# A long convolution beside a gated MLP, backward pass: halo rows moved by DMA, and one slab load placed later

## The chip, the cores and the metric

The kernel runs on one core of a Trainium2 chip. The metric is the device time of one execution in microseconds (us); lower is better. The engines are TensorE (PE in the profile, PEld for its weight loads), VectorE (DVE), ScalarE (ACT), GpSimd (POOL) and SyncE (SP), which here issues most of the DMAs ("SPq" rows are such issues).

## What is computed

The reference is the forward pass and the gradients of a block with two branches on one layer-normed input, S = 2048 positions, D = 1024 channels, F = 3584 hidden columns, all bf16.

```python
def _A_ref(q, k, v, shift_k, ssm_k, ssm_D):
    k_pad = jnp.pad(k, ((0, 0), (ks - 1, 0), (0, 0)))          # ks = 4 taps
    for t in range(ks):
        k_shift = k_shift + k_pad[:, t:t + S, :] * shift_k[:, ks - 1 - t][None, None, :]
    kv = k_shift * v
    y = ...                        # causal convolution of kv with ssm_k along S, by FFT
    y = y + kv * ssm_D[None, None, :]
    return q * y
def _B_ref(x, W_gate, W_up, W_down):
    gate = x @ W_gate;  gate = gate * (gate > 0);  h = gate * (x @ W_up)
    return h @ W_down

x = A_q
xn = _layernorm(x, axis=-1)
out = x + _A_ref(xn, A_k, A_v, ...) + _B_ref(xn, W_gate, W_up, W_down)
# returned: out, and by jax.vjp the gradients of A_q, A_k, A_v, shift_k, ssm_k, ssm_D and the three weights
```

What matters here is the gradient through the four-tap shift. With gks the gradient of k_shift, the gradient of k at position s is the sum over i of gks[s + i] * shift_k[i], i = 0 to 3. It needs the next three positions; behind the last position they are zero.

## The kernel before, in words

**The MLP branch** (class LnMlp) has four phases of large matmuls. `hidden` makes gate, up and the hidden gradients, 14 blocks of 512 columns (two halves of the rows, seven column blocks each), with weight tiles wg, wu and wdT refilled from HBM ahead of the next block (`load_gate`, `load_up`, `load_down`). The results h and the two gradients ug are stored to the HBM scratch tensors h_d and ug_d. `grad_down` makes the gradient of W_down from slabs of h (tile hs) and the output gradient (g_nat), and `grad_in` makes those of W_gate and W_up from slabs of ug (tile ugs) and the normed input (xn_nat). A slab is 2048 rows by 512 columns, 2 MB, loaded by eight DMAs of 256 KB into one of two sets of buffers (`slab`, `slab_part`, L1216 to L1230). `grad_in` runs 14 turns of 128 matmuls. At the start of turn k it asks for the slab of turn k + 1. Behind them come `out_phase` and `grad_x`, the forward output and the gradient of the input.

At the change from grad_down to grad_in the last columns of the one and the first of the other are computed by `four` (L1244): four PSUM banks are accumulated together, first over the rows 0 to 7 (blocks of 128) and then over 8 to 15. In grad_down's last `four` each g_nat block that has been read for the last time gives its buffer to an xn_nat block (`load_xn`, L1289), so the last eight xn_nat loads can be issued only when grad_down's last matmuls have run. Stores of finished tiles (wo of grad_down, wi of grad_in) are deferred by two steps (`defer`, `tick`).

**The convolution branch** (class ABranch) handles the channels in eight groups of 128. Per group it does forward and inverse transforms by matmuls, with elementwise products on VectorE. A group in time layout is a tile of 128 partitions by 19 rows by 128 channels. Partition 64u + q holds the 16 consecutive positions from 32q + 16u on in its rows 0 to 15; so the position behind the last one of a partition is row 0 of another partition: partition 64 + q for q in the first half, and q + 1 of the first half for 64 + q. Rows 16 to 18 of the tile gks are the halo: a copy of rows 0 to 2 of that next partition. `halo` (L493) fills them, and `taps` reads rows i to i + 15 for tap i. `tap_sums`, the sums for the gradient of shift_k, reads rows 0 to 15 only.

**Order.** Once the convolution branch has started (`pri.strict`), every instruction of an engine is kept in the order in which the program emits it, DMA issues on SP too. The MLP phases are generators that yield after every 8 matmuls or so with an estimated time. The convolution branch is a list of slots (`slots`, L627), each with a PE part and a VectorE part. The main loop gives it slots until their estimated times have used up what the MLP phase has yielded. In `hidden` a slot counts 1900 ns; in the dense phases (grad_down, grad_in) it counts 1900 ns with a PE part and 1250 ns without:

```python
    SLOT, DENSE = 1900, (1900, 1250)
    ...
                yield self.DENSE[p is None] if self.dense else self.SLOT
```

In the slots around the halo, gks and gv are made by VectorE, gv is stored by two DMAs on SP (`store_time`), and one slot further comes the halo, then tap_sums. The loads of the next group (vt, kp, xt and others) wait in a queue and are issued one per slot.

Of the kernel before, what the change touches and what calls it, by code (L numbers as in the profile page):

```python
# [11 lines left out]
BF16 = mybir.dt.bfloat16  # L12
F32 = mybir.dt.float32
# [4 lines left out]
P = 128  # L18
# [30 lines left out]
class ABranch:  # L49
# [81 lines left out]
    def tables(self):  # L131
        nc, con, big, pri = self.nc, self.con, self.big, self.pri
        pri.late()
        V = nc.vector
# [40 lines left out]
        for ri in range(2):  # L175
            off = lin(b32, -1024.0, 1024.0 * (1 + ri) + 2048.0, "offF%d" % ri)
            q = big.tile([P, NB1, NB1], I32, name="qF", tag="big")
# [20 lines left out]
        q = big.tile([P, 3, 8, NB1], I32, name="qI", tag="big")  # L198
# [18 lines left out]
            V.tensor_scalar(out=self.RB[:, h, :], in0=trB[:], scalar1=m[:], scalar2=None, op0=ALU.mult)  # L217

        self.ident32 = con.tile([P, 1, 32], BF16, name="ident32")
        self.NX = con.tile([P, P], BF16, name="NX")  # L220
        V.memset(self.NX[:, P - 1:P], 0.0)
        V.tensor_copy(out=self.NX[:, 0:64], in_=self.identA[:, 64:P])
        V.tensor_copy(out=self.NX[:, 64:P - 1], in_=self.identA[:, 1:64])
        for b in range(0, P, 32):
            V.tensor_copy(out=self.ident32[b:b + 32, 0, :], in_=self.identA[b:b + 32, b:b + 32])

# [265 lines left out]

    def halo(self, st):  # L493

        gks, ps = st["gks"], self.ps.tile([P, 2, 512], F32, name="ps7", tag="aps")
        self.mm(ps[:, 1, 0:3 * P], self.NX[:], gks[:, 0:3, :].rearrange("p r c -> p (r c)"))
        self.act(gks[:, 16:19, :].rearrange("p r c -> p (r c)"), ps[:, 1, 0:3 * P])

    def tap_sums(self, st):

# [126 lines left out]
    def slots(self, st, gi):  # L627
# [12 lines left out]
        q = self.cmul(H, G, True, GKV, 0)  # L640
# [7 lines left out]
        q = self.cmul(H, G, True, GKV, 1)  # L648
# [12 lines left out]
        q = self.cmul(K, G, True, G, 0)  # L661
# [13 lines left out]
        q = self.cmul(H, K, False, K, 0)  # L675
# [4 lines left out]
        gks = st["gks"] = self.ttile("gks")  # L680
# [3 lines left out]
        yield None, lambda: self.tt(gv[:, 0:16, :], gkv[:, 0:16, :], st["ksh"][:], ALU.mult)  # L684
        self.store_time(self.out_gv, st["cg"], gv)
        yield None, q
        yield lambda: self.halo(st), q
        yield lambda: self.tap_sums(st), None
        self.fetch(nx, self.load_k, self.load_taps)
        f1g = None  # L690
# [7 lines left out]
        q = self.cmul(K, G, True, G, 1)  # L698
# [5 lines left out]
        q = self.cmul(H, K, False, K, 1)  # L704
# [75 lines left out]
class LnMlp:  # L780
# [207 lines left out]
    PACE = (2100, 1350)  # L988

    def hidden(self, first, goT, load, ln, tables, Wg, Wu, Wd, g, xn_d, h_d, ug_d):  # L990


# [4 lines left out]
        for n in range(N):  # L997
# [185 lines left out]
            for sp in range(0, HS, 2):  # L1183
                self.pri.now()
                while len(gT) < min(sp + 6, HS):
                    gT.append(self.load_T(g, len(gT), "goT", HS + len(gT)))
                if ahead or sp < HS - 4:
                    if not ahead:
                        load_down(sp // 2)
                        yield from gate_up(sp)  # L1190
                    yield from grad(sp)
                elif sp == HS - 4:
                    yield from last_rows(sp)
                if ahead:
                    with self.tc.issue_after(self.stored.ins):
                        if sp in (0, 4):
                            load(6 + sp // 4)
                        if sp == 0:
                            for q in range(4):
                                load_down(q)  # L1200
                if ahead and sp + 4 < HS:
                    yield from gate_up(sp + 4)
                if n == 1 and sp in (0, 2):
                    with self.tc.issue_after(self.stored.ins):
                        load(8 + sp // 2)
                if ahead and sp == 4 or n == 1 and sp in (0, 6):
                    chunk()
                if ahead and sp == 4:
                    with self.tc.issue_after(self.ln_act.ins), self.tc.issue_after(self.ln_dve.ins):
                        tables()  # L1210
# [111 lines left out]
    def grad_in(self, ug_d, out_wg, out_wu):  # L1322
        nc, xn, nxt = self.nc, self.xn_nat, self.ugs
        turns = [(fb, w) for fb in range(self.FB) for w in (1, 0)]
        for k, (fb, w) in enumerate(turns):
            out = out_wg if w else out_wu
            self.pri.now()
            sl = self.rows_of(nxt)
            if k + 1 < len(turns):
                nf, nw = turns[k + 1]  # L1330
                nxt = self.slab(ug_d[:, nw, :], nf, "ugs", self.FB + k + 1)
            for dp in range(self.DT // 2):
                self.pri.now()
                if k == 0 and dp == 1:
                    continue
                if k == 0 and dp == 0:
                    wo = [self.e2_tile("wi") for _ in range(2)]
                    yield from self.four("ps_w", lambda i, st: xn[st][:, i * P:(i + 1) * P], lambda i, st: sl(st),
                                         lambda i: wo[i // 2][:, i % 2, :], lambda st: None)
                else:  # L1340
                    wo = [self.e2_tile("wi")]
                    for d in range(2):
                        dc = 2 * dp + d
                        ps = self.ps_tile("ps_w")
                        yield from self.gemm16(ps, lambda st: xn[st][:, dc * P:(dc + 1) * P], sl)
                        self.pri.pin(nc.scalar.copy(out=wo[0][:, d, :], in_=ps[:]))
                for i, t in enumerate(wo):
                    def store(r=(dp + i) * 256, t=t, fb=fb, out=out):
                        self.pri.pin(nc.sync.dma_start(out=out[r:r + 256, fb * 512:fb * 512 + 512].rearrange(
                            "(s p) f -> p s f", p=P), in_=t[:]))  # L1350
                    self.defer(store)
        for _ in range(3):
            self.tick()
# [259 lines left out]
```

## Time and profile before

| quantity | value |
|---|---|
| median of 4 runs | 1885.9 us (1885.24 to 1886.61) |
| the profiled execution | 1885.77 us |
| its span, first to last instruction | 1884.0 us |
| TensorE busy | 1874.7 us, 13720 matmuls |
| VectorE / ScalarE busy | 1051.7 / 613.7 us |
| DMA moved | 322.93 MB, mean 171 GB/s |
| halo products (tile NX) | 8 matmuls of 326 ns, first at 229.2 us, last at 1178.2 us |
| casts of the halo out of PSUM | 8 of 478 ns on ScalarE |
| slab loads (tile ugs) | 112 DMAs of 256 KB, 834.1 to 1247.6 us |

The profile is of one execution. Its rows give the instruction's source line, its engine and operation, the tile that it writes and those that it reads; many of the convolution branch's rows carry the line of a helper: L72 for a matmul, L76 for a cast on ScalarE, L80 for an elementwise operation on VectorE, L88 and L96 for loads and stores. In a timeline the columns are the start, the length, the instruction, and in brackets the idle time ahead of it with what ended it. Matmuls are pipelined and their ends are modelled, so two neighbours overlap in the rows.

### The profile page before, as it was taken

How to read it: one execution, taken by the hardware profiler on the slowest of the kernel's cores; microseconds unless marked ns; L12 is line 12 of the kernel's file. 1: busy time of each engine (PE TensorE's matmuls, PEld its weight loads, DVE VectorE, ACT ScalarE, POOL GpSimd, SP SyncE). 2: the span in 40 equal slices, each digit the busy share in tenths (PEclk: the TensorE clock that was granted, in tenths of full speed). 3: DMA queues.
4: the chain of work that ended last, by engine and by line, in shares of the span. 5: the costliest groups of instructions: out<-in, count | busy, mean ns of one | idle time of the engine just before them, and what ended most of it. 6: DMA issues, size and time to landing. Idle time of an engine off the chain costs nothing.

```text
span 1884.0 us, 32762 instructions
## 1 busy us (share of the span) xinstructions
PE 1874.7 (100%) x13720; PEld 853.6 (45%) x13720; DVE 1051.7 (56%) x1544; ACT 613.7 (33%) x858; POOL 14.9 (1%) x37
## 2 busy tenths in 40 slices
PE   9999999999999999999999999999999999999999
PEld 4444444444444444444444444444444544444444
DVE  6676887888698685774775856600222232222222
ACT  5654354444534445444345444311000000000000
POOL 1000000000000000000000000000000000000000
PEclk9999999999999999999999999999999999999999
DMA  9897689696577665375654452594999955555553
GB/s 252 249 231 178 140 197 227 179 212 175 144 175 208 210 160 164 96 190 190 148 150 135 117 157 80 157 296 110 243 262 243 244 123 123 123 123 123 124 123 73
DMA packets 694038, 322.93 MB, mean 171 GB/s; under 512 B 524409, under 2 KB 663425, under 8 KB 693889
## 3 DMA queue, kind: packets, MB, share of 16 engines
q1 hardware_dynamic: 683392, 299.99, 64.9%
q10 hardware_dynamic: 9216, 16.65, 2.8%
q0 software_dynamic: 1280, 4.20, 0.7%
q8 instruction: 107, 1.75, 0.4%
q14 instruction: 43, 0.34, 0.1%
HBM read 143.79 MB, written 95.44 MB: 127 GB/s over the span
## 4 chain that ended last, share of the span: by engine, by line
PE 66%; DMA 0%; SPq 0%; DVE 0%; issue 0%
PE ps_x L1469 21%; PE ps_w L1238 20%; PE ps_o L1400 10%; PE ps_d L1238 9%; PE ps L72 3%; PE ps_d L1251 1%; PE ps_h L939 0%; PE ps_u L939 0%; PE ps_r L1430 0%; DMA xn_nat<-xn_d 0%; PE ps_w L1251 0%; SPq L962 0%; PE ps_g L939 0%; DVE arena L329 0%; DVE rest L1434 0%
## 5 line engine op out<-in xcount | busy, mean ns | idle before, releaser
L1238 PE MATMUL ps_w<-ugs,xn_nat 128*128 128x512 bf16 x1728 | 383.7, 379 | 0.0
L76 ACT CAST arena<-ps 128x1024 bf16<-128x1024 f32 x288 | 277.6, 1017 | 171.4 <-PE ps L72 170.4
L939 PEld LDWEIGHTS <-xnT 128*128 128x128 bf16 x1792 | 170.5, 98 | 209.1 <-issue 8.7
L1238 PEld LDWEIGHTS <-xn_nat 128*128 128x128 bf16 x1728 | 164.3, 98 | 201.1 <-issue 10.2
L329 DVE STREAM_TRANSPOSE arena<-arena 128x1024 f32<-128x1024 f32 x96 | 179.9, 1933 | 89.9 <-ACT arena L76 88.0
L939 PE MATMUL ps_u<-wu,xnT 128*128 128x512 bf16 x896 | 206.8, 379 | 0.0
L939 PE MATMUL ps_g<-wg,xnT 128*128 128x512 bf16 x896 | 205.1, 379 | 0.7 <-ACT xnT L974 0.4
L939 PE MATMUL ps_h<-wdT,goT 128*128 128x512 bf16 x896 | 205.5, 379 | 0.0
L1487 ACT ACTIVATE w<-xn,m 128x512 f32<-128x512 bf16 x32 | 24.3, 807 | 553.0 <-issue 317.2
L1469 PE MATMUL ps_x<-wuT,guT 128*128 128x512 bf16 x896 | 198.6, 379 | 0.0
L1469 PE MATMUL ps_x<-wgT,ggT 128*128 128x512 bf16 x896 | 198.6, 379 | 0.0
L1400 PE MATMUL ps_o<-wd,hT 128*128 128x512 bf16 (+1 forms) x896 | 187.6, 372 | 0.0
L1238 PE MATMUL ps_d<-g_nat,hs 128*128 128x512 bf16 x768 | 172.0, 379 | 0.0
L1469 PEld LDWEIGHTS <-guT 128*128 128x128 bf16 x896 | 87.7, 98 | 105.7
L1469 PEld LDWEIGHTS <-ggT 128*128 128x128 bf16 x896 | 87.7, 98 | 105.5
L1400 PEld LDWEIGHTS <-hT 128*128 128x128 bf16 x896 | 87.7, 98 | 99.9
L939 PEld LDWEIGHTS <-goT 128*128 128x128 bf16 x896 | 85.5, 98 | 104.5 <-issue 4.7
L1145 ACT CAST gh<-ps_h 128x512 bf16<-128x512 f32 x112 | 65.6, 587 | 183.2 <-PE ps_h L939 176.2
L1471 DVE CUSTOM_DVE_ANT_0 gx<-ps_x,gy 128x512 f32<-128x512 f32 x32 | 22.1, 691 | 181.9 <-PE ps_x L1469 181.8
L1392 DVE TENSOR_TENSOR ya<-ya,xe 128x1024 bf16<-128x1024 bf16 x16 | 11.1, 692 | 197.4 <-DMA xe<-xn_d 197.4
L1045 DVE SCALAR_TENSOR_TENSOR ru<-ru,ps_u 128x512 bf16<-128x512 bf16 x112 | 76.5, 683 | 76.6 <-PE ps_u L939 54.8
L80 DVE TENSOR_TENSOR t<-arena 128x2048 bf16<-128x2048 bf16 x96 | 114.0, 1218 | 0.4
(149 smaller groups left out, 1332.8 us busy)
## 6 DMA issues: line engine op xcount, KB each, us to landing
ug_d<-ru SPq DMA_DIRECT2D x112, 256.0 KB, 3.4
ugs<-ug_d SPq DMA_DIRECT2D x112, 256.0 KB, 4.2
wg<-in_B_W_gate_dram SPq DMA_DIRECT2D x56, 256.0 KB, 4.2
wu<-in_B_W_up_dram SPq DMA_DIRECT2D x56, 256.0 KB, 4.7
h_d<-ht SPq DMA_DIRECT2D x112, 128.0 KB, 2.6
hs<-h_d SPq DMA_DIRECT2D x56, 256.0 KB, 4.6
out_dram<-wi SPq DMA_DIRECT2D x56, 256.0 KB, 2.5
gt<-in_grad_out_dram SPq DMA_DIRECT2D x32, 256.0 KB, 3.1
```

Of the source, the lines that this page charges most:

```text
L72: self.pri.pin(self.nc.tensor.matmul(out, lhsT=lhsT, rhs=rhs, start=start, stop=stop))
L76: self.pri.pin(self.nc.scalar.copy(out=out, in_=in_))
L80: self.pri.pin(self.nc.vector.tensor_tensor(out=out, in0=in0, in1=in1, op=op))
L329: self.pri.pin(self.nc.vector.transpose(out=df[:, c0:c0 + 32, :], in_=sf[:, c0:c0 + 32, :]))
L939: self.pri.pin(self.nc.tensor.matmul(ps[:], lhsT=xT[:, kt * P:(kt + 1) * P], rhs=w(kt), start=(kt == 0), stop=(kt == self.DT - 1)), always ...
L1045: self.pri.pin(nc.vector.scalar_tensor_tensor(out=ru[s][:, 1, :], in0=ru[s][:, 0, :], scalar=0.0, in1=ps[:], op0=ALU.is_gt, op1=ALU.mult))
L1145: self.pri.pin(nc.scalar.copy(out=gh[:], in_=ps[:]))
L1238: self.pri.pin(self.nc.tensor.matmul(ps[:], lhsT=lhsT(st), rhs=rhs(st), start=(st == 0), stop=(st == self.ST - 1)))
L1400: nc.tensor.matmul(ps, lhsT=hT[:, kt, :], rhs=self.wd[:, kt, oc], start=(kt == 0), stop=(kt == self.FT - 1))
L1469: nc.tensor.matmul(ps, lhsT=T[:, kt, :], rhs=W[:, kt, oc], start=(i == 0), stop=(i == n - 1))
L1471: V.tensor_tensor_reduce(out=gx[:, oc], in0=ps, in1=gy[:, oc], scale=1.0, scalar=0.0, op0=ALU.add, op1=ALU.add, accum_out=m[:, ob:ob + 1])
L1487: nc.scalar.activation(out=w[:, oc], in_=xn[:, oc], func=ACT.Identity, scale=m[:, 7:8], bias=m[:, 6:7])
```

## The change

The matrix NX, with which TensorE shifted rows 0 to 2 of gks by one partition in the sequence, becomes a small row of zeros. The halo rows are filled by three DMAs from SBUF to SBUF on SP: 64 partitions, 63 partitions, and the last partition from the row of zeros. The halo is no longer the PE part of its slot. It is emitted in the VectorE part, ahead of the VectorE step q of the same slot; the slot has no PE part now. In `grad_in` the request for the slab of turn 1 moves from the start of turn 0 to its step dp = 2, behind the first `four`; the other turns ask as before.

```diff
-        self.NX = con.tile([P, P], BF16, name="NX")
-        V.memset(self.NX[:, P - 1:P], 0.0)
-        V.tensor_copy(out=self.NX[:, 0:64], in_=self.identA[:, 64:P])
-        V.tensor_copy(out=self.NX[:, 64:P - 1], in_=self.identA[:, 1:64])
+        self.NX = con.tile([1, 3, P], BF16, name="NX")
+        V.memset(self.NX[:], 0.0)
...
     def halo(self, st):
 
-        gks, ps = st["gks"], self.ps.tile([P, 2, 512], F32, name="ps7", tag="aps")
-        self.mm(ps[:, 1, 0:3 * P], self.NX[:], gks[:, 0:3, :].rearrange("p r c -> p (r c)"))
-        self.act(gks[:, 16:19, :].rearrange("p r c -> p (r c)"), ps[:, 1, 0:3 * P])
+        gks = st["gks"]
+        self.load(gks[0:64, 16:19, :], gks[64:P, 0:3, :])
+        self.load(gks[64:P - 1, 16:19, :], gks[1:64, 0:3, :])
+        self.load(gks[P - 1:P, 16:19, :], self.NX[0:1, 0:3, :])
...
-        yield lambda: self.halo(st), q
+        yield None, self.both(lambda: self.halo(st), q)
...
             sl = self.rows_of(nxt)
-            if k + 1 < len(turns):
-                nf, nw = turns[k + 1]
-                nxt = self.slab(ug_d[:, nw, :], nf, "ugs", self.FB + k + 1)
             for dp in range(self.DT // 2):
+                if dp == (k == 0) * 2 and k + 1 < len(turns):
+                    nf, nw = turns[k + 1]
+                    nxt = self.slab(ug_d[:, nw, :], nf, "ugs", self.FB + k + 1)
                 self.pri.now()
```

## The prediction

> **What bounds the kernel now.** I read the page first: span, TensorE's busy time, its row in the slices, and the granted clock below it.
>
> ```profile
> span 1884.0 us, 32762 instructions
> PE 1874.7 (100%) x13720; PEld 853.6 (45%) x13720; DVE 1051.7 (56%) x1544; ACT 613.7 (33%) x858; POOL 14.9 (1%) x37
> PE   9999999999999999999999999999999999999999
> PEclk9999999999999999999999999999999999999999
> ```
>
> PE has work in every slice at the full clock, and idles 9.3 us in all. Nothing is won that doesn't take work or waits off PE, and a wait added to PE's in-order stream costs its full length. Since ends of matmuls are modelled, I count PE time from start to start. Second, the answers for the tile NX and PE's timeline at the last halo product:
>
> ```profile
> L72 PEld LDWEIGHTS <-NX x8: 97/98/98, 229.0 to 1178.0; 128*128 128x128 bf16 x8
> L72 PE MATMUL ps<-gks,NX x8: 326/326/326, 229.2 to 1178.2; 128*128 128x384 bf16 x8
> ...
> 1174.79 3.62 PE L1238 MATMUL ps_w<-ugs,xn_nat 128*128 128x512 bf16 x16
> 1178.24 0.33 PE L72 MATMUL ps<-gks,NX 128*128 128x384 bf16 x1
> 1178.40 1.89 PE L1238 MATMUL ps_w<-ugs,xn_nat 128*128 128x512 bf16 x8
> 1180.22 1.08 PE L72 MATMUL ps<-kp,gks 128*32 128x128 bf16 x64
> ```
>
> The product lasts 326 ns but takes 163 ns of the stream (1178.24 to 1178.40), since the next one starts inside it; all eight are 162 to 163 ns. Third, PE's and SP's timelines where grad_down hands over to grad_in, the place of the second edit:
>
> ```profile
> 876.38 1.47 PE L1251 MATMUL ps_w<-ugs,xn_nat 128*128 128x512 bf16 x6
> 878.00 0.39 PE L1251 MATMUL ps_w<-ugs,xn_nat 128*128 128x512 bf16 x1
> 878.69 0.39 PE L1251 MATMUL ps_w<-ugs,xn_nat 128*128 128x512 bf16 x1 [0.31 <-DMA xn_nat<-xn_d]
> 879.38 5.57 PE L1251 MATMUL ps_w<-ugs,xn_nat 128*128 128x512 bf16 x25 [0.30 <-DMA xn_nat<-xn_d]
> ...
> 868.89 4.82 SPq L962 DMA_DIRECT2D xn_nat<-xn_d  x8
> 873.81 5.91 SPq L1220 DMA_DIRECT2D ugs<-ug_d  x8
> 880.15 1.13 SPq L1318 DMA_DIRECT2D out_dram<-wo  x2
> 882.14 13.02 SPq L1349 DMA_DIRECT2D out_dram<-wi  x3
> 898.72 3.96 SPq L1220 DMA_DIRECT2D ugs<-ug_d  x8
> ```
>
> These matmuls normally start 216 ns apart. Here three steps took 0.54, 0.69 and 0.69 us: 1.27 us lost, waiting for xn_nat blocks that arrive one by one. It is the largest PE stall by a DMA in the kernel, while the slab of turn 1 is being issued behind those loads.
>
> **The change, part by part.** *Halo product removed.* Eight matmuls at 0.163 us of PE stream: 1.30 us gained, on the path. Its weight load of 98 ns lies inside the previous matmul, as the stream shows. Eight ACT casts (0.478 us, 3.8 us in all) go too; ACT is 33% busy and no engine is shown waiting for them: nothing. One PSUM buffer less per group is taken from a ring of two, so tap_sums comes one place nearer to inv_b's evictions, done several us earlier: nothing. In the tables two copies (0.173 and 0.176 us) and a memset become one memset at about 70 us, off the path.
>
> *Halo DMAs added.* Three per group on SP, 48, 47.2 and 0.75 KB. The nearest rows are the kp loads of the same sizes:
>
> ```profile
> kp<-in_A_k_dram SPq DMA_DIRECT2D x8, 48.0 KB, 5.3
> L88 SPq DMA_DIRECT2D kp<-in_A_k_dram x32: 522/712/2407, 98.6 to 1070.4; - x32
> ...
> 1176.12 1.32 SPq L96 DMA_DIRECT2D out_dram<-gv  x2
> ...
> 1173.74 1.22 DVE L80 TENSOR_TENSOR gks<-gkv,vt 128x2048 bf16<-128x2048 bf16 x1
> 1195.52 1.22 DVE L80 TENSOR_TENSOR tap<-gks,skb 128x2048 bf16<-128x2048 bf16 x1
> ```
>
> At 0.71 us each SP is held 2.1 us per group (ends: 0.9 us, three of the 0.3 us that the small final stores take, and 7.2 us, three of the slowest kp issue). SP doesn't wait for data there: the gv stores just ahead in its order already waited for a later product of the same VectorE stream. What is queued behind: stores of h, ug, wo and wi, the next group's kp, and in one group the next weights. The first halo reader is the tap at offset 1. From the last gv issue to that tap the eight groups leave 13.9 to 31.8 us. In the seventh group a slab of eight loads (1058.67 to 1064.6) lies between, which leaves some 5 us after a landing put at 1072 (issue at 1064.7, 2.1 us of issuing, 5.3 us to land). So the transfer is hidden. Without that cover VectorE would wait, and PE only after it.
>
> Here a rule of the Trainium skill speaks against the change. "DMA: Bandwidth & Descriptors", section "Rules for kernel authors", says to coalesce, since a transfer under 64 KB is mostly overhead; its section on the anatomy of a DMA puts the fixed part at about 2.0 us. Three small transfers per group in a row would be 6 us, or 48 us over eight groups, against 1.3 us saved. The trace shows even worse latency, 5.3 us at 48 KB under load, but also the 13.9 us or more of cover; the rule prices latency, and latency is not on PE's path here. I take zero; the rule would be right only if PE waited.
>
> Does the delay of SP hurt PE? The tightest weights are the wu loads at 231.57 to 234.25: the last landed at 239.13 and is used at 239.4. But load_up stands ahead of the grad_row whose yield runs the first halo, so these loads stay ahead of it. The wg loads at 542.4 are used at 555.6, and the slabs 20 us or more after issue. A 2.1 us delay is absorbed in all of them; only a 7.2 us one could reach something. Bounds on PE: 0 to +2 us. I take 0, because each queued load keeps over 5 us from its last issue to its use.
>
> *Order of slots.* The halo slot no longer has a PE step. In the dense phases (the last five groups) it then counts 1250 instead of 1900 ns, so the attention branch runs 0.65 us earlier per group, 3.25 us at its end. VectorE has room: in the last group it idles 2.73 us before the tap diagonals. Boundaries may fall one block of 8 matmuls differently; other PE hitches in this branch are 0.1 to 0.3 us each. I put it at 0, with 0.5 us either way.
>
> *Slab later.* For k = 0 the eight loads move from ahead of the first four-bank pass to behind it in SP's order. But SP follows its order, not PE's time. Between the two places it has only the two wo stores, whose data is on hand from about 869.6 (the last ACT cast); all other SP entries until 898 come after. So SP should issue wo, wo at about 873.8 and the slab right behind, some 1.4 us later than now, not 12 us. Does that free the xn_nat loads? In the semaphore records each slab issue waits for the landing of the DMA eight places before, and so tells when each xn_nat block landed: from 873.79 to 879.33, and then the slab's own from 880.09 to 885.27 at the same 0.7 us pace. Transfers are served nearly in order: the slab was behind xn_nat already, and now stores are. Bounds: 0 to 1.27 us gained; I take 0.2, near zero for that reason. Its cover remains: landing by about 887, used from 897.9. If SP did wait for PE's half turn, it would issue at 885 and end at about 891 to 896, just enough.
>
> **The sum.** The profiled execution took 1885.77 us, its span 1884.0 and 1.8 around it; the median shown is 1885.9, the same within 0.01%. 1.30 + 0.2 = 1.5 us off: 1885.9 - 1.5 = 1884.4 us.
>
> **The rivals.** (1) *The xn_nat stall goes altogether*: the slab's reads did slow the earlier loads, and small stores don't. 1.30 + 1.27 = 2.6 us: 1883.3. For it: the DMA engines are full from 875 to 885; against it, the equal landing pace. (2) *The gain is eaten*: shifted slots or a late load cost PE about what the products did, 1885.9. For it: hitches of 0.2 us at many PSUM turns; against it, the margins above. (3) *Slower: tap_sums waits for the halo DMAs*, if the wait is drawn over the whole gks tile. They stand one slot earlier, and PE would stop until they land. From each last gv issue plus 6.5 us (two issues and 5.3 us of landing) to tap_sums' present start gives 5.6, 11.4, 5.2, 4.7, 7.9, 7.4, 2.7 and 3.7 us: 48.6 in all, 1885.9 - 1.5 + 48.6 = 1933. It decides from 0.16 us of wait per group, and shows as slower from 0.66. Against it: tap_sums reads rows 0 to 15, the halo is rows 16 to 18, and the arena, a single tile, is written by ACT (238.20) while VectorE and PE read other parts of it (237.05, 237.52): waits go by region.
>
> **How the numbers follow.** Forecast 60%, rival 1 15%, rival 2 12%, rival 3 or a smaller wait of its kind 13%. What this kernel's measurement tells from no change is about 0.2%, 3.8 us: below 1882.1 or above 1889.7. The most that I can count as gain is 2.6 us, and 0.5 us of slot shift doesn't reach it, so faster keeps only 7% for what I don't see; slower has rival 3 and 3% more, 16%; same 77%. The range runs from 1882.6 (rival 1 and the slot shift) to 1887.4 (the forecast, +2 us from a late load and 1 us of shift and scatter), and leaves out most of rival 3.
>
> **What would show it.** Right: no NX matmul and no gks cast; 24 new SP issues landing before the tap at offset 1; tap_sums directly after a matmul without a DMA wait; wo stores at about 874, the slab at about 875; PE hitches near 878 still some 1 us. Wrong: a wait of PE for gks or of VectorE for the halo, a weight or slab landing after its first use, or no hitch near 878.

## The result, and the profile after

The kernel after takes 1882.73 us (median of 40 runs, 1882.14 to 1884.61), the kernel before beside it 1885.61 us (58 runs): 2.9 us less, a ratio of 0.9984 with a 95% interval of 0.998 to 0.9989. The gain is real, and twice the 1.5 us forecast; the time lies at the low end of the range that the prediction gave. It is still under the 0.2% that the prediction took as the bound of "same". The page after:

```profile
span 1880.6 us, 32785 instructions
PE 1873.3 (100%) x13712; PEld 852.8 (45%) x13712; DVE 1051.5 (56%) x1542; ACT 610.0 (32%) x850; POOL 14.9 (1%) x37
PE   9999999999999999999999999999999999999999
PEclk9999999999999999999999999999999999999999
```

Eight matmuls fewer and the same clock. PE's busy time fell by 1.4 us, which is about the eight products, but the span fell by 3.4 us. So about 2 us of this profile's gain (some 1.6 us of the medians') came from places where PE stood still or ran slowly, and not from removed work. The rows of the tiles NX and gks, and PE's timeline at the last group:

```profile
L88 SPq DMA_DIRECT2D gks<-gks x16: 520/890/1871, 234.8 to 1172.1; - x16
L88 SPq DMA_DIRECT2D gks<-NX x8: 579/591/597, 236.4 to 1173.5; - x8
...
1165.81 7.72 PE L1237 MATMUL ps_w<-ugs,xn_nat 128*128 128x512 bf16 x35
1173.45 1.08 PE L72 MATMUL ps<-kp,gks 128*32 128x128 bf16 x64
```

The 24 halo issues are there. tap_sums (kp, gks) follows a large matmul directly with no wait, although the last halo DMA is issued at 1173.5, no earlier than tap_sums starts. The whole group also stands 6.8 us earlier than before (1173.45 against 1180.22), twice what the span lost: some 3.4 us are the branch's own shift, close to the 3.25 us that the prediction worked out. The handover from grad_down to grad_in, PE and then SP:

```profile
867.19 0.42 PE L72 MATMUL ps<-kvt,R 32*64 32x512 bf16 x8
867.54 6.43 PE L1250 MATMUL ps_w<-ugs,xn_nat 128*128 128x512 bf16 x29
873.91 0.42 PE L72 MATMUL ps<-kvt,R 32*64 32x512 bf16 x8
874.26 6.00 PE L1250 MATMUL ps_w<-ugs,xn_nat 128*128 128x512 bf16 x27
...
857.50 1.30 SPq L96 DMA_DIRECT2D y_d<-yt  x2
858.89 1.15 SPq L1317 DMA_DIRECT2D out_dram<-wo  x1
860.13 3.05 SPq L961 DMA_DIRECT2D xn_nat<-xn_d  x5
863.27 1.97 SPq L96 DMA_DIRECT2D out_dram<-ghn  x2
865.35 4.98 SPq L961 DMA_DIRECT2D xn_nat<-xn_d  x8
870.53 1.00 SPq L1317 DMA_DIRECT2D out_dram<-wo  x2
871.81 5.19 SPq L1219 DMA_DIRECT2D ugs<-ug_d  x8
```

The slow steps near 878 are gone: 27 matmuls take 6.00 us, 26 steps of 0.216 us and the last one's 0.38. The slab's issue stands right behind the two wo stores, as forecast. But also the last eight xn_nat loads start at 865.35, that is 1.5 us ahead of grad_down's last matmul (866.88). Before they started at 868.89, 0.3 us behind it (868.57). That is a larger move than PE's own, so the slab need not be what freed them. (The description of the kernel before says that the eight can be issued only when grad_down's last matmuls have run. They need not wait so long: each waits for its own g_nat block.) The yt stores, which stand ahead of xn_nat loads in SP's order, left 2.9 us earlier. Before, SP and then ScalarE at the same place:

```profile
856.38 2.05 SPq L962 DMA_DIRECT2D xn_nat<-xn_d  x3
860.44 1.30 SPq L96 DMA_DIRECT2D y_d<-yt  x2
863.02 4.41 SPq L962 DMA_DIRECT2D xn_nat<-xn_d  x5
...
858.48 1.93 ACT L76 CAST yt<-ps 128x1024 bf16<-128x1024 f32 x2 [4.32 <-PE ps L72]
```

SP stood idle for 2.0 us ahead of the yt stores (858.43 to 860.44), until ScalarE's casts into yt ended at 860.41. After, it went on to them within 0.1 us.

### The profile page after: what moved, and what is told of

The parts are those of the page before. It is cut to its first block, busy times and chain, and to the rows that moved or that the text cites. A ratio compares the mean times of both kernels' runs of the same rounds, so it can differ in the third digit from the quotient of the medians.

```text
span 1880.6 us, 32785 instructions
## 1 busy us (share of the span) xinstructions
PE 1873.3 (100%) x13712; PEld 852.8 (45%) x13712; DVE 1051.5 (56%) x1542; ACT 610.0 (32%) x850; POOL 14.9 (1%) x37
## 4 chain that ended last, share of the span: by engine, by line
PE 66%; DVE 0%; issue 0%
PE ps_x L1468 21%; PE ps_w L1237 20%; PE ps_o L1399 10%; PE ps_d L1237 9%; PE ps L72 3%; PE ps_d L1250 1%; PE ps_w L1250 1%; PE ps_h L938 0%; PE ps_u L938 0%; PE ps_r L1429 0%; PE ps_g L938 0%; DVE arena L327 0%; DVE rest L1433 0%; PE ps L766 0%; PE ps L769 0%
```

## The experiments

Two theories stood against each other. S: the slab's loads had slowed the xn_nat loads, and moving them removed the stall. T: the shorter slot (1250 instead of 1900 ns, no PE part) moved the convolution branch earlier against the MLP. Its yt stores then no longer hold SP back from the xn_nat loads. A third reason, H, came from the same shift: slots that follow each other more or less closely cost PE more or less. Each run below was measured beside the kernel before; the intervals are those of the ratio of the two times. Most of them are about 1.7 us wide to either side, so a part of a microsecond is read from the profiles, one of each run.

**The slab alone.**

```diff
 # before, with only:
-            if k + 1 < len(turns):                  # ahead of the loop over dp
+                if dp == (k == 0) * 2 and k + 1 < len(turns):
```

> The kernel before with the second edit alone: the slab of turn 1 is asked for behind the first four-bank pass; the halo product and its slot stay. Theory S (the slab's loads slowed the xn_nat loads, the edit frees them): the three slow steps near 878 us vanish, 1.27 us off, about 1884.4. Theory T (the shift of the slots did it, not the slab): the hitches near 878 stay at about 1.3 us, the slab's issues come about 1.3 us later behind the two wo stores, and the time is that of before within 0.3 us.

Measured: 1885.48 us against 1885.36 for before, ratio 1.0 (0.9991 to 1.0009). Waits of PE's weight loads (the sum in us, the number, the longest), in before and in this run, and this run's SP timeline:

```profile
PEld L1251 <- DMA xn_nat<-xn_d: 2.0, 4, 0.6
PEld L1251 <- DMA xn_nat<-xn_d: 1.7, 3, 0.6
...
860.48 1.30 SPq L96 DMA_DIRECT2D y_d<-yt  x2
868.57 4.95 SPq L962 DMA_DIRECT2D xn_nat<-xn_d  x8
873.62 1.16 SPq L1318 DMA_DIRECT2D out_dram<-wo  x2
874.96 6.01 SPq L1220 DMA_DIRECT2D ugs<-ug_d  x8
```

The slab is 1.15 us later, the wo stores go first, and the wait for xn_nat stays (1.7 us of weight loads, 2.0 before). S fails in this setting.

**The slot cost alone**, the product kept:

```diff
-        yield lambda: self.halo(st), q
+        yield None, self.both(lambda: self.halo(st), q)     # halo() still the product
```

> The kernel before with the halo product kept, but its slot counted 1250 instead of 1900 ns in the dense phases (the call stands in the VectorE part of the slot); the slab as before. Theory T: the convolution branch runs up to two blocks of 8 matmuls earlier, its yt and ghn stores leave SP ahead of the last xn_nat loads, the stall near 878 vanishes (1.27 us) and the PE hitches at neighbouring slots fall by about 0.8 us: 2.0 us off, about 1883.6. Theory S: no change in the stall; at most the hitches, 0 to 0.8 us off.

Measured: 1884.17 us, 1.2 us off (0.9984 to 1.0001, which just includes no gain); the profiled span fell by 1.6 us. No work was removed. The xn_nat waits halve:

```profile
PEld L1251 <- DMA xn_nat<-xn_d: 1.0, 2, 0.6
...
858.18 1.30 SPq L96 DMA_DIRECT2D y_d<-yt  x2
866.49 6.16 SPq L962 DMA_DIRECT2D xn_nat<-xn_d  x8
```

The loads start 1.1 us ahead of grad_down's last matmul. A part of the stall is left; issuing the eight took 6.2 us here, 4.8 before. The full 2.0 us expected was not reached.

**The halo alone, as in the change.** After, with the slab as before.

> The first edit alone, as in the kernel after (halo by three DMAs, slot counted 1250 ns); the slab as before. Theory T: all of the gain is here, 1.30 for the products, 1.27 for the stall and about 0.8 for hitches, 2.9 to 3.4 us off, the same as the kernel after. Theory S: 1.30 and 0.8, but the stall near 878 stays: about 2.0 us off.

Measured: 1882.44 us, 2.9 us off, ratio 0.9983 (0.9975 to 0.9992): all of the change's gain without its second edit. Of the stall, 0.2 us of weight-load wait is left.

**The halo by DMA with the long slot.**

```diff
-        yield lambda: self.halo(st), q
+        yield (lambda: None), self.both(lambda: self.halo(st), q)     # halo() by three DMAs
```

> The halo by three DMAs, but its slot still counted 1900 ns (an empty PE part), the slab as before. Both theories: the eight products' 0.163 us each, 1.30 us off, and the stall near 878 stays (T because the slots are not shifted, S because the slab is not moved): about 1884.3. If the three DMAs cost SP or PE anything, less than 1.30 is gained.

Measured: 1884.03 us, 1.33 us off (0.9983 to 1.0001), the eight products to within what this can tell. The three DMAs cost nothing visible. That 1.33 meets 1.30 so closely is partly luck: in the profile 1.87 us are gone, and 0.38 of them come from a shorter stall at the handover (table below). Against the halo alone, which differs only in the slot's cost, this version is 1.6 us slower.

**Both edits with the long slot.**

> Both edits, but the halo's slot still counted 1900 ns. Theory T: the same as the halo by DMA with the long slot, 1.3 to 1.9 us off, with hitches near 878 left, since the slab's place does nothing. Theory S: about 1 us better than that, 2.6 to 2.9 us off, no hitch near 878.

Measured: 1884.57 us, 0.66 us off (0.9988 to 1.0005), no better than without the slab's move; the weight loads still wait for xn_nat:

```profile
PEld L1250 <- DMA xn_nat<-xn_d: 2.6, 3, 1.5
```

So the slab's place removes no stall here either. T expected 1.3 to 1.9 us off, and the result is less. The stall of this one profile is longer than in the halo-by-DMA version; how much of that is the slab's place and how much scatter of the DMA was not separated.

**The yt stores later**, the direct test of T, on the kernel before:

```diff
         yield None, flh
-        self.store_time(self.y_d, st["cg"], st["yt"])
         yield None, tk
         yield None, tk
         yield self.inv_b_chan(st, 1), tk
+        self.store_time(self.y_d, st["cg"], st["yt"])
```

> The kernel before with one move: the two stores of yt are emitted three steps later (behind inv_b_chan), so that in SP's order they no longer stand ahead of the xn_nat loads 3 to 7; halo product, slots and slab as before. Theory T (SP is late with the xn_nat loads because it waits for yt in between): xn_nat loads 3 to 7 are issued about 3 us earlier, the last eight start 1.5 to 2.4 us ahead of grad_down's end instead of 0.3 us behind it, and the stall of 1.27 us near 878 shrinks to under 0.4: about 1.0 us off, 1884.4. Theory S (traffic of the slab right behind): no change.

Measured: 1884.73 us, 0.5 us off (0.9988 to 1.0005): less than expected, and by the time alone not told from no change. What it shows of T stands in the profile, at the handover (SP, then PE):

```profile
860.29 2.61 SPq L962 DMA_DIRECT2D xn_nat<-xn_d  x5
863.00 1.30 SPq L96 DMA_DIRECT2D y_d<-yt  x2
866.02 2.28 SPq L96 DMA_DIRECT2D out_dram<-ghn  x2
868.40 4.42 SPq L962 DMA_DIRECT2D xn_nat<-xn_d  x8
...
877.05 7.08 PE L1251 MATMUL ps_w<-ugs,xn_nat 128*128 128x512 bf16 x32
```

The loads 3 to 7 go ahead of yt, the last eight start 0.8 us ahead of grad_down's end (1.5 to 2.4 were expected), and the 32 matmuls run at full pace: no hitch is left. In the table below that is -1.28 us between grad_down's end and turn 0's end. The rest was given back in `hidden`: this profile is 0.68 us behind before the dense phases, and has a PE wait for a wu load (0.6 us) that before didn't show. Whether the moved stores cause that or it is scatter was not tested. The lead of the last eight is not all that counts: 0.8 us sufficed here, where 1.1 us in the slot cost alone left a part of the stall. Issuing the eight took 4.4 us here and 6.2 us there; what sets that pace stayed open.

**Pace: slots two blocks apart**, to test H. In the timeline of before, the same 32 products in two places:

```profile
757.55 0.63 PE L72 MATMUL ps<-arena,FW 64*32 64x256 bf16 x32
758.11 1.90 PE L1238 MATMUL ps_d<-g_nat,hs 128*128 128x512 bf16 x8
759.94 0.91 PE L72 MATMUL ps<-arena,FW 64*32 64x256 bf16 x32
```

The second stands one block of eight matmuls behind the first and takes 0.28 us more. After, ScalarE and PE in such a pair:

```profile
910.75 1.93 ACT L76 CAST arena<-ps 128x1024 bf16<-128x1024 f32 x2 [1.45 <-PE ps L72]
...
910.29 0.42 PE L72 MATMUL ps<-hn,R 32*64 32x512 bf16 x8
910.64 1.90 PE L1237 MATMUL ps_w<-ugs,xn_nat 128*128 128x512 bf16 x8
912.48 0.97 PE L72 MATMUL ps<-arena,IA 32*64 32x128 bf16 x64
```

The first slot fills both PSUM buffers of the branch's ring; the casts out of them end at 912.68, after the next slot has begun at 912.48. The same 64 products take 0.76 us elsewhere. Inside this burst PE stands still and goes on 0.05 us behind the end of the second cast; in the other six of the kernel after it is 0.05 to 0.06 us as well. Counted start to start over the dense phases, before has ten such neighbours, 2.59 us together, and after has seven, 1.76 us. Not every close pair loses: bursts of 64 matmuls of 128 columns (ps<-arena,FW) 2.4 to 2.5 us behind the slot before, and tap_sums 1.98 us behind the halo product, ran at their usual length. The slot costs of after were then changed so that a slot with PE work, one without and the next with PE work take two blocks of 1730 ns:

```diff
-    SLOT, DENSE = 1900, (1900, 1250)
+    SLOT, DENSE = 1900, (2210, 1250)        # and, in another run, (2260, 1200)
```

> The kernel after with the dense slot costs 2210 and 1250 ns: a slot with PE work, one without and the next with PE work then lie 3460 ns apart, two blocks of 1730. Theory H (a slot's matmuls cost 0.21 to 0.28 us more when they stand one block behind the slot before, waiting for their PSUM buffers): such neighbours fall from 7 in the kernel after to 3 or fewer, about 1 us off against the kernel after (near 1881.7). The branch ends some 20 us later; if loads for the output phase come too late for it, it is slower instead.

> The same with 2260 and 1200 ns: again 3460 together, but a slot without PE work is shorter than the 1.22 to 1.38 us that its VectorE step takes. Theory H: as few neighbours as with 2210 and 1250, so the same gain of about 1 us over the kernel after, unless VectorE falls behind; then PE waits for VectorE and it is slower than that by 1 us or more.

Measured with 2210 and 1250: 1880.75 us, 4.5 us off before (0.9976, 0.9966 to 0.9985), about 1 us better than expected; all seven neighbours vanish. With 2260 and 1200: 1882.32 us. There the neighbours are gone as well, but the yt stores now fall just ahead of the last eight xn_nat loads, which start only at 866.29, 0.1 us behind grad_down's last matmul, and the stall is back:

```profile
PEld L1250 <- DMA xn_nat<-xn_d: 1.9, 3, 0.7
...
864.89 1.30 SPq L96 DMA_DIRECT2D y_d<-yt  x2
866.29 5.58 SPq L961 DMA_DIRECT2D xn_nat<-xn_d  x8
```

The expectation had named VectorE falling behind as what could eat the gain; it was the loads.

**The pace on the kernel before, and the better version beside after.**

> The kernel before with nothing but the dense slot costs 2210 and 1250 ns instead of 1900 and 1250; halo by the product, slab as before. Theory H: the ten neighbour hitches of the dense phases (2.6 us together) vanish, and by theory T the stall of 1.27 us near 878 goes too if yt's stores now fall behind the xn_nat loads: 2.6 to 3.9 us off, about 1881.4 to 1882.6, though none of the change is in it. If the gain of this pace needed the change's halo or slab, little is gained.

> The kernel after itself, beside the next on the same chip: about 1882.6, 2.9 us below the kernel before.

> The kernel after with the dense slot costs 2210 and 1250 once more, now beside the kernel after on one chip: by theory H 1.7 us below it (the seven neighbour hitches), about 1880.9.

Measured on one chip, with before at 1885.42 us: before with the new slot costs 1881.93 us, ratio 0.9983 (0.9974 to 0.9992); after 1882.42 us, 0.9986 (0.9977 to 0.9994); after with the new slot costs 1880.65 us, 0.9976 (0.9967 to 0.9986). So two numbers in the pacing, with no part of the change, gain 3.5 us, within the 2.6 to 3.9 expected and as much as the change; no close neighbour loses time in that profile, and no wait for xn_nat is left. On top of the change they gain 1.8 us more, where H said 1.7. The runs of the two after versions don't overlap (1882.16 to 1884.02, and 1880.4 to 1881.5), so this version beats both kernels. A second profile of the kernel after, from this set, has 0.4 us of weight-load wait for xn_nat, where the first has none.

**Where the time went**, from the starts of ScalarE's evictions and, in the last column, of PE's first matmul into ps_o, in us against before (negative is earlier):

| kernel | last ps_h | last wo (grad_down's end) | eighth wi (turn 0's end) | first ps_o |
|---|---|---|---|---|
| slab alone | +0.05 | +0.05 | -0.06 | -0.06 |
| slot cost alone | -0.03 | -1.00 | -1.73 | -1.60 |
| halo, long slot | -0.66 | -1.00 | -1.38 | -1.87 |
| both edits, long slot | -0.75 | -1.09 | -0.29 | -0.79 |
| halo alone | -0.62 | -1.91 | -3.18 | -3.54 |
| after | -0.39 | -1.69 | -2.96 | -3.32 |
| yt stores later | +0.68 | +0.67 | -0.61 | -0.61 |
| after, 2210 and 1250 | -0.59 | -2.54 | -2.82 | -5.05 |
| after, 2260 and 1200 | -0.33 | -2.42 | -0.61 | -3.49 |
| before, 2210 and 1250 | +0.41 | -2.16 | -4.11 | -3.35 |

Behind the first ps_o no kernel gains or loses over 0.1 us. In the last three rows the two middle columns can't be read as a stall: with the other slot costs a burst of 0.9 us (ps<-RB,arena) stands behind grad_down's end instead of ahead of it, and the eighth wi waits on ScalarE behind a slot's casts. For after the parts add up: 0.39 ahead of the dense phases, five products of 0.163 (0.81), neighbours 0.83 (2.59 less 1.76), and the stall 1.27: 3.30 of the 3.32 measured. The first term and the stall are read from the table itself, so what this sum tests is the rest: 1.66 us measured against 0.81 and 0.83. The rest is 1.65 for the halo alone, 0.83 for the halo with the long slot, where only the products are gone (ten neighbours as before), and 0.84 for the slot cost alone, where only three neighbours are gone.

## Why the prediction was half right

*Right: the bound and the products.* PE's stream was the measure, and 0.163 us per product gave 1.30 us. The halo with the long slot measured 1.33, and in its profile the five products of the dense phases were worth 0.83 us, 0.81 by this price.

*Right: the halo DMAs are hidden.* In the after profile an issue takes 0.93 us on average, so SP is held 2.8 us per group, not 2.1 but inside the bounds. The 0.71 us were the median of a row in which half of the kp loads are of 256 KB; its small ones alone took 0.90 us on average. From the last issue to the first tap that reads the halo the groups leave 8.4 to 28.0 us, and no VectorE wait for it shows. The Trainium skill's rule on transfers under 64 KB ("DMA: Bandwidth & Descriptors", "Rules for kernel authors") spoke against the change, and this case's runs charge nothing for it that they can tell: whatever the latency is, it is not on PE's path. The prediction's 48 us, an estimate, took its 2.0 us from the page's section on DMAs that GpSimd issues; these are issued by SP, so it was not the right price even for the latency. Rival 3 (tap_sums waits for the DMAs) is excluded: the last group's rows above show no wait, and no wait of PE in that profile is for gks.

*Right: the slab.* SP issued it directly behind the wo stores, and the move alone measured 0 where 0.2 was taken. Rival 1 (1883.3) had the right fate for the stall with the wrong cause: the hitch vanished with the slab left where it was (yt stores later, and nearly so with the halo alone, where only 0.2 us of weight-load wait was left).

*Wrong: "Order of slots", put at 0 with 0.5 us either way.* This is the step that failed. It asked only whether VectorE has room for the earlier slots, not what else moves with the slots. Two things did. First, the branch's yt stores stand in SP's order between the xn_nat loads; with the slots earlier by one to three blocks of matmuls there, SP no longer waits for yt's data, and the stall of 1.27 us goes. Second, the spacing of slots changed, and with it how often PE arrives at PSUM buffers that ScalarE has not emptied: 0.83 us. The slot cost alone measured 1.2 us in the medians (1.60 in the profile) and, with the halo by DMA in both, 1.6 us (the halo alone against the long slot), where the prediction had 0. Products and slot cost together measured 2.9 (3.54 in the profile). At the handover the slot cost alone takes 0.73 us off, the halo with the long slot 0.38, and both together all 1.27 (the two middle columns of the table).

The "other PE hitches of 0.1 to 0.3 us" were seen and left inside the half microsecond either way. They had a cause, a count and a price: ten at about 0.26 us.

## What to carry to other kernels

Where two streams share an engine by estimated times, an edit that changes a slot's class is an edit of the schedule: look for what rides with the slots, their stores in the DMA queue above all, and price that beside the work removed. Before moving the transfer that stands behind a late load, look at what stands ahead of it in the issue order; a store waiting for its data there can hold the load back. Small equal hitches on a full engine are worth counting: here ten of them, 2.59 us together and removed by two pacing numbers, were worth more than the eight products.

## What was not expected of the hardware

A slot's matmuls that begin 2.2 to 2.5 us behind the slot before lost 0.21 to 0.29 us of PE time, in most of the close pairs, to two casts that take 1.93 us together (128x1024, 1.02 us each). Two blocks apart they lost nothing. The time that SP needs for an issue hardly follows the size: from SBUF to SBUF 0.89 us as a median for 48 and 47.2 KB, and 0.59 us even for the single row of 0.75 KB; the kp loads of 256 KB before had 0.71.
